# One plain chunk of tokens less, Strassen steps of 1024 tokens, and late weights decoded among the attention heads

## The chip, the core and the metric

The kernel runs on one core of one Trainium2 chip. The metric is the device time of one execution in microseconds (us); lower is better. All arithmetic is in float32, built from pairs of rounded parts as told below.

## What is computed

Causal attention with a decay term for 8 batches of 8 heads, 576 positions and 64 numbers a head, followed by a mixer: one MLP along the positions, one along the channels. Cut to what matters:

```python
scores = q @ k.T / 8 + cum[i] - cum[j]          # cum: running sum of log f; causal
x = (softmax(scores) @ v)                       # 8 batches x 576 tokens x 512 channels
u = x + (relu(x.T @ w_tok1) @ w_tok2).T         # 576 -> 256 -> 576 along the tokens
out = u + relu(u @ w_ch1) @ w_ch2               # 512 -> 1536 -> 512 along the channels
```

There are 8 x 576 = 4608 tokens in the last line. The 1536 hidden channels are 12 tiles of 128.

## The kernel before

**Numbers.** A float32 operand of a matmul is split into a rounded high part and the remainder, the low part (`hi_act`, `lo_dve`, `lo_pool`). A product is then three matmuls: high by high, low by high, high by low. The weights arrive as 64-bit floats; decoding (`decode`, L792) makes float32 of them by one ScalarE operation (L810), a shift (L814) and an OR (L818) on VectorE, and then splits them.

**Heads.** A loop over 64 heads computes scores, softmax and the product with v; after every four heads of a batch `mixer` (L1635) runs the token MLP, and the part of the channel MLP that belongs to the first two hidden tiles (`F1=2`). TensorE, VectorE, ScalarE and GpSimd all work here; GpSimd splits k, q and v and scales the probabilities. The mixed values u and the partial results of the first two hidden tiles go to DRAM (`u_d`, `part_d`).

**Late weights.** The other 10 tiles of w_ch1 and 10 of w_ch2 (`w1r`, `w2r`) don't fit beside the heads' buffers. They are decoded when those buffers are given up (`rest` L867; `gate0`, `gate1`), at the end of the heads.

**Plain chunks.** `CONV=2` chunks of 512 tokens go through these 10 hidden tiles in the ordinary way: `up` (L1238) 12 matmuls of 512 columns for a tile, `down` (L1266) 12 more. Beside them the weights are made ready for the last stage. For each of five pairs of hidden tiles, high and low part of a weight are added again (`prep` L1331, `prep2` L1382), four sums of quarters are formed and split, the sums for w2 are stored in DRAM (`sums_d`), and so are the plain quarters of w2 (`keep` L1373, `quads_d`).

**Strassen steps.** The other 3584 tokens go in four steps of 896 (`big` L1438; `HT=448` is half a step). A step multiplies 2 x 2 blocks with 7 products in place of 8, once up and once down: 7 products x 5 pairs x 6 matmuls each way. The blocks of w1 stay in SBUF; those of w2 are loaded again for every product (`product` L1553), in part into the memory that `w2r` held. The running results R start as the partial results from DRAM plus u (L1472, L1477); for the first step two of their four buffers are those from which the last chunk's output is stored.

**Order.** Nothing is scheduled on the chip: a planner (`Plan`) puts all operations in order ahead of time by priorities (the tables `PR`, by kind of operation, and `prio`), durations and buffers, and each engine works through its own list in order. Operations marked `port=True` on VectorE and all of GpSimd's are planned so that they don't overlap. All DMAs are issued from one queue, SP's, in order.

## Time and profile before

| what | value |
|---|---|
| median of 3 runs | 1040.6 us (1038.58 to 1043.64) |
| the profiled execution, its own time | 1045.64 us |
| its span, first to last instruction | 1043.5 us |
| TensorE busy | 1028.1 us, 99% |
| VectorE busy | 809.2 us, 78% |
| ScalarE busy | 689.8 us, 66% |
| GpSimd busy | 420.2 us, 40% |
| DMA | 192.60 MB, mean 185 GB/s |
| granted TensorE clock, mean | 0.998 of full |

In the profile PE is TensorE's matmuls, PEld its weight loads, DVE is VectorE, ACT is ScalarE, POOL is GpSimd, SP is the queue that issues DMAs. Matmuls overlap, so the distance between the starts of two of them tells their pace, not the duration of one. GpSimd's 420 us all lie in the first 570 us.

### The profile page before, as it was taken

The page shows a single profiled execution, that of the slowest core. Times are in us where ns is not written, and L with a number is a line of the kernel's source. Part 1 is how long each engine was busy: PE and PEld are TensorE (multiplying, and loading weights), DVE is VectorE, ACT ScalarE, POOL GpSimd, SP SyncE. Part 2 cuts the span into 40 slices and gives each one's busy share as a digit, 9 for nine tenths or more (in the row PEclk, how much of TensorE's full clock was granted, in tenths as well). Part 3 has the DMA queues.
Part 4 walks back from the last instruction along what each step waited for, and adds up shares of the span by engine and source line. Part 5 has one row for each costly group of instructions (what it writes and reads, how often), then busy time and mean ns, then how long its engine had stood idle before and what let it go on. Part 6 is the DMA issues. An engine that isn't in the chain of part 4 may idle for free.

```text
span 1043.5 us, 19849 instructions
## 1 busy us (share of the span) xinstructions
PE 1028.1 (99%) x6489; PEld 930.0 (89%) x6489; DVE 809.2 (78%) x1970; ACT 689.8 (66%) x1719; POOL 420.2 (40%) x528
## 2 busy tenths in 40 slices
PE   9999999999999999999999999999999999999998
PEld 7578999999999999999998888879998999999997
DVE  6798888788787868878998895545976886686694
ACT  6888888888888878888996542235454654644652
POOL 6579878778778676977932000000000000000000
PEclk9999999999999999999999999999999999999999
DMA  8765667465564654555657845152582485277054
GB/s 246 246 206 194 217 226 256 162 217 197 189 204 174 219 185 163 196 196 198 225 163 247 267 148 159 47 170 83 167 273 86 135 249 182 81 246 221 18 167 155
DMA packets 101606, 192.60 MB, mean 185 GB/s; under 512 B 14032, under 2 KB 45520, under 8 KB 100480
## 3 DMA queue, kind: packets, MB, share of 16 engines
q1 hardware_dynamic: 101504, 191.34, 55.4%
q8 instruction: 52, 0.85, 0.3%
q14 instruction: 50, 0.41, 0.1%
HBM read 100.16 MB, written 37.49 MB: 132 GB/s over the span
## 4 chain that ended last, share of the span: by engine, by line
PE 87%; DMA 4%; DVE 4%; ACT 2%; issue 1%; SPq 1%; DVEq 0%; ACTq 0%
PE bank L1041 10%; PE bank L985 6%; PE bank L1584 5%; PE bank L1585 5%; PE bank L1586 5%; PE bank L1522 5%; PE bank L1523 5%; PE bank L1524 5%; PE pair L985 3%; PE pair L1123 3%; PE pair L1125 3%; PE pair L1277 2%; PE pair L1279 2%; PE pair L1113 2%; PE pair L1278 2%; DMA dd<-in_w_ch 2%
## 5 line engine op out<-in xcount | busy, mean ns | idle before, releaser
L1027 POOL TENSOR_SCALAR pr<-pr,rec 64x64 f32<-64x64 f32 (+4 forms) x320 | 164.7, 530 | 65.6 <-DVE rec L1020 32.9
L719 ACT ACTIVATE p<-bank 128x384 fp32r<-128x384 f32 (+3 forms) x300 | 130.6, 473 | 20.3 <-PE bank L1041 17.5
L1041 PE MATMUL bank<-ident,pr 128*128 128x128 f32 (+1 forms) x960 | 141.4, 274 | 1.4 <-DVE low L728 0.4
L999 ACT ACTIVATE pr<-bank,nmin 64x64 f32<-64x64 f32 (+3 forms) x256 | 118.2, 468 | 18.4 <-DVE nmin L992 15.7
L1041 PEld LDWEIGHTS bank<-ident,pr 128*128 128x128 f32 (+1 forms) x960 | 106.1, 130 | 19.7 <-issue 2.9
L992 DVE CUSTOM_DVE_ANT_0 bank<-bank,mask 128x320 f32<-128x320 f32 (+3 forms) x256 | 106.8, 433 | 9.3 <-PE bank L985 5.8
L728 DVE TENSOR_TENSOR p<-bank,p 128x384 fp32r<-128x384 f32 (+1 forms) x180 | 105.0, 591 | 10.4 <-ACT p L719 8.7
L985 PE MATMUL bank<-k 128*128 128x320 f32 (+1 forms) x480 | 82.8, 302 | 0.9 <-DVE low L728 0.5
L1584 PE MATMUL bank<-ring,w2r 128*128 128x448 f32 x220 | 80.9, 368 | 2.0 <-DVE h L1539 2.0
L1585 PE MATMUL bank<-ring,w2r 128*128 128x448 f32 x220 | 80.8, 367 | 0.0
L1586 PE MATMUL bank<-ring,w2r 128*128 128x448 f32 x210 | 77.2, 367 | 0.0
L1125 PE MATMUL pair<-p,vv 128*128 128x512 f32 x240 | 76.9, 322 | 0.0
L719 ACT ACTIVATE ring<-xt 128x448 fp32r<-128x448 f32 (+2 forms) x99 | 59.2, 611 | 22.2 <-PE bank L1585 5.2
L911 POOL TENSOR_TENSOR hl<-raw,hl 128x1152 fp32r<-128x1152 f32 x27 | 72.1, 2670 | 1.8
L1123 PE MATMUL pair<-p,vv 128*64 128x512 f32 x240 | 70.4, 334 | 0.0
L728 DVE TENSOR_TENSOR low<-bank,p 64x512 fp32r<-64x512 f32 (+1 forms) x120 | 52.6, 445 | 17.7 <-ACT p L719 15.3
L985 PEld LDWEIGHTS bank<-k 128*128 128x128 f32 (+1 forms) x480 | 62.1, 176 | 4.4 <-ACT pr L999 1.0
L999 ACT ACTIVATE pr<-pair,nmin 128x576 f32<-128x576 f32 x64 | 47.3, 739 | 20.5 <-DVE nmin L992 18.7
L728 DVE TENSOR_TENSOR ring<-xt,ring 128x448 fp32r<-128x448 f32 (+1 forms) x62 | 38.3, 629 | 24.6 <-ACT ring L719 22.9
L992 DVE CUSTOM_DVE_ANT_0 pair<-pair,mask 128x576 f32<-128x576 f32 x64 | 48.9, 764 | 7.0 <-PE pair L985 6.9
L725 POOL TENSOR_TENSOR ring<-xt,ring 128x576 fp32r<-128x576 f32 x32 | 45.8, 1440 | 19.8 <-ACT ring L719 19.4
L722 POOL TENSOR_SCALAR p<-low 64x576 fp32r<-64x576 f32 x60 | 40.4, 673 | 32.2 <-DVE low L728 25.2
(203 smaller groups left out, 3177.9 us busy)
## 6 DMA issues: line engine op xcount, KB each, us to landing
k<-hl SPq DMA_DIRECT2D x180, 288.0 KB
w2r<-sd SPq DMA_DIRECT2D x80, 256.0 KB
raw<-in_qk SPq DMA_DIRECT2D x60, 288.0 KB
w2r<-qd SPq DMA_DIRECT2D x60, 256.0 KB
vr<-in_v SPq DMA_DIRECT2D x32, 320.0 KB
ud<-xt SPq DMA_DIRECT2D x8, 1152.0 KB
pd<-part SPq DMA_DIRECT2D x32, 288.0 KB
dd<-in_w_ch SPq DMA_DIRECT2D x12, 512.0 KB
```

The lines of the kernel that those rows point to most:

```text
L719: nc.scalar.activation(out, in_, func, scale=scale)
L728: nc.vector.tensor_tensor(out, in_, asf(hi), op=ALU.subtract)
L985: nc.tensor.matmul(ps[:m, of : of + w], k[:, 0, i0 : i0 + m], k[:, 1, j0 : j0 + w], start=(x == 0), stop=(fq or x == 1))
L992: nc.vector.tensor_tensor_reduce(x, x, E["mask"][:m, a : a + w], -1.0 / D**0.5, 3e38, op0=ALU.add, op1=ALU.min, accum_out=E["nmin"][sm][:m ...
L999: nc.scalar.activation(at(pr)[:m, poff[t] : poff[t] + w], at(buf)[:m, of : of + w], AF.Exp, bias=E["nmin"][sm][:m, t : t + 1], scale=-1.0, ...
L1027: nc.gpsimd.tensor_scalar(x, x, r, 0.0, op0=ALU.mult, op1=ALU.add)
L1041: nc.tensor.transpose(out, at(pr)[:, poff[i] + start[j] : poff[i] + end[j]], E["ident"])
L1123: nc.tensor.matmul(x[:D], at(vv)[:, v0 + j, :D], at(pb)[:, 1, c0 : c0 + w], start=False, stop=last)
L1125: nc.tensor.matmul(x, at(vv)[:, v0 + j, :], at(pb)[:, 0, c0 : c0 + w], start=False, stop=last)
L1584: nc.tensor.matmul(o_, wh[:, ms], h_, start=first and pr == 0, stop=False, skip_group_check=not first)
L1585: nc.tensor.matmul(o_, wl[:, ms], h_, start=False, stop=False, skip_group_check=not first)
L1586: nc.tensor.matmul(o_, wh[:, ms], l_, start=False, stop=pr == PH - 1, skip_group_check=not first)
```

## The change

It has two parts. `CONV` goes from 2 to 1 and `HT` from 448 to 512: one chunk of 512 tokens is left, and the four steps have 1024 tokens each. And the late weights are decoded among the heads, from the tenth head on, in buffers of the scratch memory `dd`: a pair of w1 tiles is decoded and stored unsplit in DRAM (`g_d`); a pair of w2 tiles is decoded, split and stored (`w2_d`), and its four sums are formed, split and stored at once (`sums_d`). Behind the heads the w1 tiles are loaded and split, the w2 tiles are loaded as they are, and `prep` loads its pairs from `g_d` in place of adding high and low part. `keep` and `quads_d` go; the steps read quarters of w2 out of `w2_d`. The body of `prep2` is otherwise the same. Fewer buffers are left for the steps' split values (16 for 18), and some buffers of the steps lie elsewhere. The tables `PR` have new numbers throughout, and are left out here:

```diff
-HT = 448
-CONV = 2
+HT = 512
+CONV = 1
...
-    def decode(prio, loads, w, hi, lo, tok, late=None):
-        rb, gb = Buf("d_raw"), Buf("d_g")
+    def bits(prio, loads, w, rb, gb, out, wr, dur):
...
-            dma(prio - 1.0, lambda a=(rows, cols, src): ld(*a), nb / len(loads), dur=470 if late else 600, wr=[(rb, i)], bufs=[rb])
+            dma(prio - 1.0, lambda a=(rows, cols, src): ld(*a), nb / len(loads), dur=dur, wr=[(rb, i)], bufs=[rb])
...
+    def prep2(pr, g, prio):
+        e = Buf("pd")
...
+                dma(
+                    prio + 0.6, lambda j=j, z=z, src=src: nc.sync.dma_start(E["sums_d"][pr][:, 2 * j : 2 * j + 2, z, :], src()),
+                    P * C * 4, dur=400, rd=rd, wr=[("st", pr, 2 * j + n, z) for n in (0, 1)], bufs=[g if z else e],
+                )
...
-        def rest(i, which):
+        def rest(pr, w):
             def go(prio):
-                if which == 1:
-                    fs = sl((F1 + i) * P, P)
-                    loads = [(full, sl(c * P, P), w_ch1[sl(c * P, P), fs]) for c in range(NC)]
-                else:
-                    loads = [(full, sl(0, C), w_ch2[sl((F1 + i) * P, P), :])]
-                key = f"w{which}r"
-                decode(
-                    prio, loads, C, lambda: E[key][i][:, 0, :], lambda: E[key][i][:, 1, :], (key, i),
-                    late=f"gate{int(i >= PAIRS0)}",
-                )
+                gb = Buf(f"sg{w}")
+                for j in (0, 1):
+                    i = 2 * pr + j
+                    if w == 1:
+                        fs = sl((F1 + i) * P, P)
+                        loads = [(full, sl(c * P, P), w_ch1[sl(c * P, P), fs]) for c in range(NC)]
+                    else:
+                        loads = [(full, sl(0, C), w_ch2[sl((F1 + i) * P, P), :])]
+                    bits(prio + 1.2 * j, loads, C, Buf("s_raw"), gb, lambda j=j: at(gb)[:, j, :], (gb, j), 470)
+                if w == 1:
+                    dma(prio + 2.4, lambda: nc.sync.dma_start(E["g_d"][pr], asf(at(gb))), P * C * 8, dur=400, rd=[(gb, 0), (gb, 1)], wr=[("g", pr)], bufs=[gb])
+                    return
+                for j in (0, 1):
+                    hb = Buf("sh")
+                    p.op("ACT", d_act(C, False), prio + 2.4, lambda j=j, hb=hb: hi_act(at(hb)[:, 0, :], asf(at(gb)[:, j, :])), rd=[(gb, j)], wr=[(hb, 0)], bufs=[gb, hb])
+                    p.op(
+                        "DVE", d_dve(C), prio + 2.4, lambda j=j, hb=hb: lo_dve(at(hb)[:, 1, :], asf(at(gb)[:, j, :]), at(hb)[:, 0, :]),
+                        rd=[(gb, j), (hb, 0)], wr=[(hb, 1)], bufs=[gb, hb], port=True,
+                    )
+                    dma(prio + 2.4, lambda i=2 * pr + j, hb=hb: nc.sync.dma_start(E["w2_d"][i], asf(at(hb))), P * C * 8, dur=400, rd=[(hb, 0), (hb, 1)], wr=[("w2d", 2 * pr + j)], bufs=[hb])
+                prep2(pr, gb, prio + 3.6)

...
-        third = [rest(i, w) for i in range(F2) for w in (1, 2)]
+        third = [rest(pr, w) for pr in range(F2 // 2) for w in (1, 2)]
...
-        fn(HB + 2 + PRM["DEC3"] * i + (OFF["dec3"] if i < 2 * PAIRS0 else 0.0))
+        fn(10 + 5.2 * i)
+    for i in range(F2):
+        b, gate = Buf("lg"), f"gate{int(i >= PAIRS0)}"
+        pr_ = HB + 2 + 0.5 * i
+        dma(pr_ - 1, lambda b=b, i=i: nc.sync.dma_start(at(b), E["g_d"][i // 2][:, i % 2, :]), P * C * 4, dur=400, rd=[("g", i // 2), ("st", F2 // 2 - 1, 3, 1)], wr=[b], bufs=[b])
+        p.op("ACT", d_act(C, False), pr_, lambda b=b, i=i: hi_act(E["w1r"][i][:, 0, :], at(b)), rd=[b, gate], wr=[(("w1r", i), "h")], bufs=[b])
+        p.op("DVE", d_dve(C), pr_, lambda b=b, i=i: lo_dve(E["w1r"][i][:, 1, :], at(b), E["w1r"][i][:, 0, :]), rd=[b, (("w1r", i), "h")], wr=[(("w1r", i), "l")], bufs=[b], port=True)
+        dma(pr_, lambda i=i: nc.sync.dma_start(asf(E["w2r"][i]), E["w2_d"][i]), P * C * 8, dur=400, rd=[("w2d", i), gate], wr=[(("w2r", i), z) for z in "hl"])
...
-    p.op("POOL", 1, HB + 3, lambda: None, rd=[((f"w{w}r", i), z) for w in (1, 2) for i in range(F2) for z in "hl"], wr=["gated"])
...
-        for j in (0, 1):
-            rd = [((key, i0 + j), z) for z in "hl"] + [("old", key, i0 + j, z) for z in "hl"] + ["gated"]
-            p.op(
-                eng, d(C), prio, lambda j=j: tt(at(g)[:, j, :], asf(E[key][i0 + j][:, 0, :]), asf(E[key][i0 + j][:, 1, :]), ALU.add),
-                rd=rd, wr=[(g, q) for q in QUADS if pos[q][0] == i0 + j], bufs=[g], port=True,
-            )
+        dma(prio - 6, lambda: nc.sync.dma_start(at(g), E["g_d"][pr]), P * C * 8, dur=400, rd=[("g", pr), ("st", F2 // 2 - 1, 3, 1)], wr=[(g, q) for q in QUADS], bufs=[g])
...
-    def keep(pr):
-        for i in (2 * pr, 2 * pr + 1):
-            rd = [(("w2r", i), z) for z in "hl"]
-            for n, hf in ((0, 0),) if i % 2 == 0 else ((1, 0), (2, 1)):
-                dma(
-                    late + PRM["P2"][pr], lambda i=i, n=n, hf=hf: nc.sync.dma_start(E["quads_d"][pr][:, n], asf(E["w2r"][i][:, :, hf * HW : (hf + 1) * HW])),
-                    P * C * 4, dur=650, rd=rd, wr=[("kept", pr, n)],
-                )
...
-        for j in (0, 1):
-            rd = ["gated"] + [(("w2r", i0 + j), z) for z in "hl"]
-            p.op(
-                eng, d(C), prio, lambda j=j: tt(at(g)[:, j, :], asf(E["w2r"][i0 + j][:, 0, :]), asf(E["w2r"][i0 + j][:, 1, :]), ALU.add),
-                rd=rd, wr=[(g, q) for q in QUADS if pos[q][0] == i0 + j] + [("recon", i0 + j)], bufs=[g], port=True,
-            )
...
-    for pr in range(PH):
-        keep(pr)
-    for pr in reversed(range(PH)):
-        prep2(pr, ENG[PRM["E2"][pr]], late + PRM["P2"][pr])
...
-    for nm, a, b, fn in (("gater", 8, 10, lambda: E["swap2"](1)), ("gatew", 0, 8, lambda: None)):
-        p.op("POOL", 1, HB + 3, fn, rd=["gatee", *(("kept", i // 2, n) for i in range(a, b) for n in range(3))], wr=[nm, *((("w2r", i), z) for i in range(a, b) for z in "hl")])
+    for nm, a, b, fn in (("gater", 7, 10, lambda: E["swap2"](1)), ("gatew", 0, 7, lambda: None)):
+        p.op("POOL", 1, HB + 3, fn, rd=["gatee"], wr=[nm, *((("w2r", i), z) for i in range(a, b) for z in "hl")])
...
                 if blk[0] == "A":
-                    tk = [("kept", pr, j)]
+                    i, hf = quad(2, pr, blk[1:])
+                    tk, src = [("w2d", i)], lambda i=i, hf=hf: E["w2_d"][i][:, :, hf * HW : (hf + 1) * HW]
                 else:
-                    tk = [("st", pr, j, z) for z in (0, 1)]
-                d_ = "quads_d" if blk[0] == "A" else "sums_d"
+                    j = dict(S3=0, S1=1, S4=2, S2=3)[blk]
+                    tk, src = [("st", pr, j, z) for z in (0, 1)], lambda j=j, pr=pr: E["sums_d"][pr][:, j]
                 dma(
-                    pp - 16, lambda w=w, d_=d_, pr=pr, j=j: nc.sync.dma_start(asf(at(w)).rearrange("p (z a) -> p z a", z=2), E[d_][pr][:, j]),
+                    pp - 16, lambda w=w, src=src: nc.sync.dma_start(asf(at(w)).rearrange("p (z a) -> p z a", z=2), src()),
                     P * C * 4, dur=650, rd=tk + ["gatew"] * (s == 0), wr=[w], bufs=[w],
...
-    k["tr"] = [(("ring", i),) for i in range(12)] + [(("w2r", i, z),) for i in (5, 6, 7) for z in (0, 1)]
+    k["tr"] = [(("ring", i),) for i in range(12)] + [(("w2r", i, z),) for i in (5, 6) for z in (0, 1)]
     k["tr0"] = k["tr"][:8]
-    k["gw"] = [dd_units(5 * i, 4) for i in (0, 2)]
-    k["pd"] = [tuple(x for i in range(4) for x in dd_units(5 * i + 4, 1))]
+    k["s_raw"] = [dd_units(4 * i, 4) for i in (0, 1)]
+    k["sg1"] = [dd_units(4 * i, 4) for i in (2, 3, 4)]
+    k["sg2"] = [dd_units(8, 4)]
+    k["sh"], k["pd"] = [dd_units(12, 4)], [dd_units(16, 4)]
+    k["lg"] = [dd_units(i, 2) for i in (0, 2, 10, 12)]
...
-    E["quads_d"] = [dram.tile([P, 3, 2, HW], F32, name=f"qd{i}") for i in range((NF - F1) // 2)]
+    E["g_d"] = [dram.tile([P, 2, C], F32, name=f"gd{i}") for i in range((NF - F1) // 2)]
+    E["w2_d"] = [dram.tile([P, 2, C], F32, name=f"wd{i}") for i in range(NF - F1)]
```

## Rows read from the trace of the kernel before

**Rows 1.** The profile's page: span, and busy time of each engine.
```profile
span 1043.5 us, 19849 instructions
PE 1028.1 (99%) x6489; PEld 930.0 (89%) x6489; DVE 809.2 (78%) x1970; ACT 689.8 (66%) x1719; POOL 420.2 (40%) x528
```
**Rows 2.** Busy by stage: stretch, length, busy (instructions), clock, DMA share, GB/s.
```profile
130.00:546.00 416.00, 415.31 (x3200) 393.34 (x3200) 349.09 (x1023) 351.35 (x976) 318.12 (x391) 1.00 0.57 198
546.00:579.30 33.30, 31.20 (x244) 30.02 (x243) 29.78 (x52) 23.13 (x48) 6.11 (x4) 1.00 0.71 236
579.30:690.20 110.90, 110.56 (x487) 90.58 (x487) 74.91 (x156) 35.49 (x79) 0.00 (x0) 1.00 0.44 144
690.20:1038.50 348.30, 345.65 (x1680) 316.10 (x1679) 251.74 (x421) 175.39 (x332) 0.00 (x0) 1.00 0.52 164
```
**Rows 3.** Timeline in a plain chunk: start, duration, instruction; 21 matmuls between.
```profile
654.65 0.39 PE L1257 MATMUL bank<-ring,w1r 128*128 128x512 f32 x1
...
659.64 0.39 PE L1258 MATMUL bank<-ring,w1r 128*128 128x512 f32 x1
```
**Rows 4.** Timeline in a Strassen step; 20 matmuls between.
```profile
895.04 0.36 PE L1524 MATMUL bank<-w2r,w1r 128*128 128x448 f32 x1
...
899.29 0.36 PE L1524 MATMUL bank<-w2r,held 128*128 128x448 f32 x1
```
**Rows 5.** Busy in three stretches of 26 us, the engines as in rows 2.
```profile
416.00:442.00 26.00, 25.88 (x196) 23.28 (x195) 22.96 (x67) 22.54 (x61) 23.67 (x31) 1.00 0.58 198
520.00:546.00 26.00, 26.00 (x202) 24.73 (x201) 24.55 (x64) 24.70 (x62) 11.52 (x19) 1.00 0.52 165
988.00:1014.00 26.00, 26.00 (x129) 24.00 (x128) 25.35 (x47) 13.93 (x27) 0.00 (x0) 1.00 0.41 127
```
**Rows 6.** Instructions grouped by line and shape, VectorE: count, busy us, mean ns.
```profile
L818 DVE SCALAR_TENSOR_TENSOR dd<-dd 128x512 uint32<-128x512 uint32 x22 | 16.0, 737 | 0.3
L814 DVE TENSOR_SCALAR dd<-dd 128x512 uint32<-128x512 uint32 x22 | 11.1, 509 | 3.1 <-ACT dd L810 3.1
L1388 DVE TENSOR_TENSOR dd<-dd 128x256 f32<-128x256 f32 x20 | 8.2, 421 | 0.1
L728 DVE TENSOR_TENSOR dd<-dd 128x256 fp32r<-128x256 f32 x20 | 7.6, 421 | 0.0
L728 DVE TENSOR_TENSOR w2r<-dd,w2r 128x512 fp32r<-128x512 f32 x10 | 6.9, 685 | 0.8 <-ACT w2r L719 0.7
```
**Rows 7.** The same view, ScalarE.
```profile
L810 ACT ACTIVATE dd<-dd 128x512 f32<-128x512 f32 x22 | 14.4, 668 | 4.6 <-DMA dd<-in_w_ch 4.1 <-DVE dd L818 0.4
L719 ACT ACTIVATE dd<-dd 128x256 fp32r<-128x256 f32 x20 | 7.5, 410 | 7.6 <-DVE dd L1388 4.8 <-DVE dd L728 2.6
L719 ACT ACTIVATE w2r<-dd 128x512 fp32r<-128x512 f32 x10 | 6.3, 629 | 3.5 <-DVE dd L818 3.5
```
**Rows 8.** Timeline, GpSimd and VectorE, 557 to 562 us.
```profile
557.60 1.43 POOL L725 TENSOR_TENSOR ring<-xt,ring 128x576 fp32r<-128x576 f32 x1 [11.83 <-ACT ring L719]
559.21 1.42 POOL L725 TENSOR_TENSOR ring<-xt,ring 128x576 fp32r<-128x576 f32 x1 [0.17 <-ACT ring L719]
...
558.33 1.00 DVE L814 TENSOR_SCALAR dd<-dd 128x512 uint32<-128x512 uint32 x1
559.36 1.82 DVE L818 SCALAR_TENSOR_TENSOR dd<-dd 128x512 uint32<-128x512 uint32 x1
```
**Rows 9.** Chain that ended last, end of the heads: start, us, what.
```profile
553.96 3.56 DMA qd<-w2r
...
577.20 5.72 DMA dd<-in_w_ch
```
**Rows 10.** First step: timeline of VectorE and TensorE, and the busy table behind it.
```profile
700.38 1.09 DVE L1477 TENSOR_TENSOR part<-part,xt 128x896 f32<-128x896 f32 x1 [2.18 <-DMA part<-pd]
...
702.11 0.44 PE L1584 MATMUL bank<-ring,w2r 128*128 128x448 f32 x1 [2.01 <-DVE h L1539]
...
703.00:707.00 4.00, 4.00 (x14) 3.55 (x13) 3.16 (x6) 1.56 (x4) 0.00 (x0) 0.60 0.73 238
```

More of the change, by code (lines that the diff above doesn't have):

```diff
@@ L501 @@
     START = dict(PE=3000, DVE=900, ACT=1900, POOL=1810, SP=700)
-    FIFO = ("ring", "xt", "part", "pr", "hl", "k1", "k2", "vv", "raw", "vr", "p34", "p2", "p1", "p0", "low", "hid", "d_raw", "d_g", "tr", "tr0", "gw", "pe", "pd", "wp", "gt12", "gt22", "xu", "qf", "f34", "f2", "f1", "f0")
+    FIFO = ("ring", "xt", "part", "pr", "hl", "k1", "k2", "vv", "raw", "vr", "p34", "p2", "p1", "p0", "low", "hid", "d_raw", "d_g", "tr", "tr0", "s_raw", "sg1", "sg2", "sh", "lg", "pe", "pd", "wp", "gt12", "gt22", "xu", "qf", "f34", "f2", "f1", "f0")
     GROUP = dict(ringx="ring")
@@ L825, in decode @@
-        p.op(
-            "DVE" if late or PRM["ED"] else "POOL", d_dve(w) if late or PRM["ED"] else d_ptt(w), prio, lambda: (lo_dve if late or PRM["ED"] else lo_pool)(lo(), asf(tl()[2]), hi()),
-            rd=[gb, (tok, "h")], wr=[(tok, "l")], bufs=[gb], port=True,
-        )
+        p.op("ACT", d_act(w, False), prio, s1, rd=rd, wr=[wr], bufs=[rb, gb])
+        p.op("DVE", d_dve(w, True), prio, s2, wr=[wr], bufs=[gb], port=True)
+        p.op("DVE", d_dve(w), prio, s3, rd=rd, wr=[wr], bufs=[rb, gb], port=True)
@@ new lines, in decode, with quad @@
+    def decode(prio, loads, w, hi, lo, tok):
+        rb, gb = Buf("d_raw"), Buf("d_g")
+        g = lambda: at(gb)[:, :w]
+        bits(prio, loads, w, rb, gb, g, gb, 600)
+        p.kinds.setdefault("s6", f"k{len(p.kinds)}")
+        p.op("ACT", d_act(w, False), prio, lambda: hi_act(hi(), asf(g())), rd=[gb], wr=[(tok, "h")], bufs=[gb])
+        p.op("POOL", d_ptt(w), prio, lambda: lo_pool(lo(), asf(g()), hi()), rd=[gb, (tok, "h")], wr=[(tok, "l")], bufs=[gb], port=True)
+    def quad(w, pr, q):
+        a, b = int(q[0]) - 1, int(q[1]) - 1
+        return (2 * pr + a, b) if w == 1 else (2 * pr + b, a)
@@ L1987, in swap @@
             for w in (1, 2):
-                pool = tp if w == 2 and i >= 8 else wp
+                pool = tp if w == 2 and i >= 7 else wp
                 E[f"w{w}r"].append(pool.tile([P, 2, C], F32R, name=f"w{w}r{i}"))
         if x == 0:
-            spare = [wp.tile([P, HT], F32, name=f"spare{i}") for i in range(2)]
+            spare = wp.tile([P, HT], F32, name="spare")
             wp.tile([P, 8], F32, name="even1")
@@ L2007, in swap2 @@
             E["H11"] = {tuple(("hid", i) for i in range(PRM["n_hid"])): [tp.tile([P, HT], F32, name=f"h11{i}") for i in range(PH)]}
+            E["H21"][(("hx", 0),)].append(tp.tile([P, HT], F32, name="h212"))
         else:
@@ L2010, in swap2 @@
                 E["R" + q] = {(("w2r", 8 + i),): tp.tile([P, 2 * HT], F32, name=f"r{q}")}
+            E["H21"][(("hx", 0),)].extend(tp.tile([P, HT], F32, name=f"h21{i}") for i in (3, 4))
     top = {}
```

301 lines of the change are left out of this document (145 added, 156 removed).

## The prediction

> **What bounds the kernel now.** I read the busy table first [rows 1]: TensorE is busy 99% of the 1043.5 us span, and no other engine passes 78%. That share is an average and "busy" includes overlapped matmuls, so the next view is the busy table by stage [rows 2]. The reader is to see four stages there. The heads at full pace run from about 130 to 546 us: 3200 matmuls in 416 us, 0.130 us each, TensorE busy 415.3, but VectorE 349.1 (84%), ScalarE 351.4 (84%) and GpSimd 318.1 (76%) beside it. The tail of the heads is 33.3 us. The two plain chunks take 110.9 us, and the four Strassen steps 348.3 us with 1680 matmuls; GpSimd does nothing in both, and VectorE is at 68% and 72%. The granted clock is full in all of them. So TensorE is the bound everywhere, in the heads with little room on the others, after them with much.
>
> Then I read the pace of an undisturbed stream in the timeline. From the 512-column matmul at 654.65 to the one at 659.64 there are 22 steps: 4.99 / 22 = 0.2268 us each [rows 3]. From the 448-column matmul at 895.04 to the one at 899.29 there are 21: 4.25 / 21 = 0.2024 us [rows 4]. 480 x 0.2268 = 108.9 of the 110.9 us of the plain chunks, and 1680 x 0.2024 = 340.0 of the 348.3 us of the steps: both stages are their matmuls, with 2 and 8 us lost.
>
> **The change in matmuls.** A plain chunk is 12 matmuls for the up product and 12 for the down product for each of 10 hidden tiles, 240 of 512 columns. One goes: 240 x 0.2268 = 54.4 us off. A step has 7 products x 5 pairs x 6 matmuls, twice, 420, and four steps 1680, before and after; each grows from 448 to 512 columns: 1680 x (0.2268 - 0.2024) = 41.0 us on. The sum is **-13.4 us**, all on TensorE, which is the path in both stages. It rests on a 512-column matmul in a step running as it does in a chunk: same weight loads, same one bank, so I take it.
>
> [...]
>
> **What the wider step asks of the others.** One column costs VectorE about (685 - 421) / 256 = 1.03 ns [rows 6], so 64 columns add 66 ns to each of the 421 instructions of the steps, some 28 us on 251.7, against 41 on 348.3 for TensorE: its share stays at 72%. Nothing is charged for it. The stretch from 988 to 1014 us had VectorE at 25.35 of 26 us and still passed 129 matmuls [rows 5].
>
> **What moves into the heads.** For each of 20 late weight tiles the three bit operations now run among the heads; so do the split of the 10 w2 tiles, and for five pairs four subtractions and four splits of 256 columns. On VectorE: 20 x 0.737 + 20 x 0.509 (the bits) + 10 x 0.685 (low parts) + 20 x 0.421 + 20 x 0.421 (sums and their low parts) = 14.7 + 10.2 + 6.9 + 8.4 + 8.4 = **48.6 us** in 90 instructions [rows 6]. On ScalarE: 20 x 0.668 + 10 x 0.629 + 20 x 0.410 = 27.9 us [rows 7]. If all of it falls in the 416 us (I subtract nothing for the few decodes that already run at their end), VectorE goes to 397.7 us, 95.6%, and ScalarE to 379.3, 91%. Is that still cover? The nearest row is 520 to 546 us, VectorE 24.55 and ScalarE 24.70 of 26, with 202 matmuls, the mean being 200 [rows 5]: at 94% nothing was lost. Against it speaks 416 to 442, VectorE 22.96 and GpSimd 23.67, with 196: 4 short, about 0.5 us. If all sixteen windows became like that one, 8.3 us would go. Below zero it can't cost, as the change takes no matmul and no evacuation out of the heads. I take the middle, **+4 us**, and keep 0 and 8.3.
>
> All 90 are instructions on SBUF operands, and there is a reason for caution. At 558.33 us a shift took 1.00 us and at 559.36 an OR took 1.82, against means of 0.51 and 0.74; both ended about one ordinary duration after a GpSimd instruction did, the second of these running from 559.21 for 1.42 [rows 8]. So such an instruction can sit out a GpSimd one, and GpSimd is busy 76% of the heads. [...]
>
> **DMA and the SP queue in the heads.** 10.5 MB of raw weights move there, and 13.1 MB of stores are added or moved (5 of 512 KB for the w1 sums' source, 10 of 512 KB for w2, 20 of 256 KB for the sums): 23.6 MB in 416 us, 57 GB/s on 198 and about 0.16 on a DMA share of 0.57. 236 GB/s at 0.71 stands in the next stage [rows 2], so there is room; 85 more issues go through SP, each store waiting there for VectorE with the heads' k and raw loads queued behind it, and TensorE waits for those. The planned order hides it as long as VectorE keeps its place; the cost is zero if so, and part of the second rival if not.
>
> **The end of the heads.** VectorE is busy 29.8 of 33.3 us there, with decoding [rows 2]. That load goes: 244 matmuls at the heads' 0.130 us would take 31.7, so up to 1.6 us could come back. What comes instead is a chain: last store of the sums, load of the decoded w1 tile, its high part, its low part, first matmul. A store took 3.56 us and a load up to 5.72 [rows 9]; with 0.63 and 0.69 for the split that is 10.6 us, and VectorE stands still for what of it isn't covered, with the last head work queued behind. Bounds -1.6 and +5 (half the chain, if TensorE has matmuls in hand for the other half); I take **0**, since the 244 matmuls of the tail mostly belong to heads and mixer and don't wait for late weights.
>
> **One chunk as cover.** A pair of tiles is wanted every 24 x 0.2268 = 5.4 us and brings 0.79 MB, 145 GB/s, under the 236 of the tail. VectorE has, in 54.4 us, some 22 instructions of 0.69, 10 low parts and 40 half-width ones: 15.2 + 6.9 + 16.8 = 38.9 us, 71%. The rebuilding additions and 15 stores vanish; five reloads of 512 KB take their place. I charge nothing. At the first step TensorE waited 2.0 us for a VectorE that waited for the partial sums, and the clock then fell to 0.60 of full for 4 us, 14 matmuls instead of 20, some 1.2 us more [rows 10]. The changed kernel has the same loads behind the same output stores, so this stays: bounds -3.2 and +4, taken **0**. The w2 quarters are read back in two runs instead of one for each row, which no row prices; they are prefetched, so nothing.
>
> **Sum.** -13.4 + 4 + 0 + 0 = -9.4 us. The profiled execution took 1045.6 us, 2.1 of it outside the span, and lies 5.0 over the median of 1040.6, so the difference goes on the median: **1031 us**.
>
> **Rivals.**
> First, *all hidden, and the joints come clean*: heads 0, tail -1.6, the first step's stall gone, -3.2: 1040.6 - 13.4 - 4.8 = 1022. For it: 202 matmuls at 94% VectorE. Against: no stage gets less tight but the tail.
> Second, *VectorE becomes the bound of the heads through the shared port*, the slower case. If each of the 90 waits as the pair did (0.49 and 1.08 over the mean, 0.79) whenever GpSimd is busy, 90 x 0.79 x 0.76 = 54 us. The most VectorE shows anywhere is 25.35 of 26, so 405.6 of 416; it is at 397.7, so it decides from 8 us of added waits, and the gain is gone at 8 + 13.4 - 4, some 17 us of them. At half the bound, 27 us: 27 - 8 = 19 us, plus the 4 already charged: 1040.6 - 13.4 + 23 = 1050. For it: the two long rows, and 90 instructions where that stretch has nearly none now. Against: without the long one the other 21 ORs of this size average (22 x 0.737 - 1.82) / 21 = 0.685 us, the same as a low part; the planned order sets them into GpSimd's gaps.
> Third, *the joints stall*: +5 at the tail and +4 at the first step, 1040, with half the cover in front of the same loads.
> Fourth, *a step's matmul costs by its columns alone*: 0.2024 x 512 / 448 = 0.2313 us, so 1680 x 0.0289 = 48.6 on and a sum of -5.8: 1040.6 - 5.8 + 4 = 1039. Against: a 512-column stream with the same loads runs at 0.2268. [...]
>
> **Chances.** Forecast 0.53 (1027 to 1036), first rival 0.13, second 0.17, third 0.12, fourth 0.05. Range 1021 to 1047: it holds the forecast, the third and fourth, most of the first and the lower edge of the second. 0.5% is 5.2 us, about what a measurement of this kernel can tell from no change. Faster (under 1035.4): 0.13 and most of the forecast, 0.64. Same: the rest of the forecast, the fourth and most of the third, 0.19. Slower: 0.17.
>
> **What would show it.** Right: 240 fewer 512-column matmuls and 1680 at 0.227 us in the steps, steps of some 95 us, one chunk of some 55 us; heads still passing 198 or more matmuls in 26 us with VectorE near 95%. Wrong: fewer than 195 there, long shifts and ORs ending just after a GpSimd instruction (second rival); idle TensorE between the last head and the first chunk matmul, with VectorE waiting for a load (third); a spacing in the steps other than 0.227 (fourth). The prediction falls if the heads end more than 10 us later than before.

## The result, and the profile after

The changed kernel takes **1030.9 us** (median of 4 runs, 1030.01 to 1032.01); the kernel before took 1042.1 (median of 4: the three runs that the forecast started from, and one more of 1044.39). The ratio is 0.9896, with a 95% interval from 0.9863 to 0.9929: faster by about 1%, some 11 us. Forecast were 1031 and a gain of 9.4; against the median of 1040.6 that the forecast started from, the gain is 9.7. In the groups of runs with the experiments the median of the kernel before is 1039.4 to 1040.6. That the time came out nearly to the point is luck, as the stages show.

The page of the changed kernel, to be read against [rows 1]: the span, the busy table, and the shares of the chain that ended last.

```profile
span 1029.7 us, 19321 instructions
PE 1015.0 (99%) x6241; PEld 882.0 (86%) x6241; DVE 804.5 (78%) x1928; ACT 695.8 (68%) x1705; POOL 422.2 (41%) x528
PE 75%; DVE 7%; ACT 6%; DMA 4%; POOL 3%; issue 3%; SPq 2%; ACTq 0%; POOLq 0%; DVEq 0%
```

TensorE is still busy 99%, so the page alone doesn't tell where anything went. The table by stage does. It has the stages of [rows 2]: start, heads at full pace, their tail, the one plain chunk, the four steps (from:to, length, then busy us and instructions of TensorE, weight loads, VectorE, ScalarE, GpSimd, granted clock, DMA share, GB/s).

```profile
0.00:130.00 130.00, 125.28 (x877) 98.86 (x878) 101.86 (x317) 103.43 (x288) 96.40 (x134) 0.99 0.69 225
130.00:558.00 428.00, 423.04 (x3213) 394.06 (x3212) 375.64 (x1101) 363.78 (x1013) 319.68 (x391) 1.00 0.69 240
558.00:586.40 28.40, 27.72 (x218) 26.90 (x217) 19.29 (x38) 17.46 (x35) 6.12 (x4) 1.00 0.77 277
586.40:643.20 56.80, 56.80 (x260) 47.37 (x259) 25.44 (x52) 16.96 (x38) 0.00 (x0) 1.00 0.33 109
643.20:1025.70 382.50, 381.99 (x1682) 314.77 (x1680) 281.62 (x421) 194.22 (x332) 0.00 (x0) 1.00 0.51 158
```

Against [rows 2], profiled execution against profiled execution (spans 1043.5 and 1029.7, 13.9 less before rounding): by the starts of the matmuls, the first of the chunk comes at 586.4 where it came at 579.3, **+7.2**; from it to the first of the steps are 56.9 us where there were 111.0, **-54.1**; from that to the last of the steps 382.1 where there were 348.3, **+33.8**; behind it 0.8 less. The forecast had +4, -54.4 and +41.0. The sum came right through errors of opposite sign: the heads cost more, the steps less. The experiments look for both.

Inside the +7.2 the heads are later still. The last of 768 score matmuls, the fourth of the group in each of these lines, starts at 541.7 instead of 529.1, **12.6 us** late (before, then the changed kernel):

```profile
528.74 0.73 PE L985 MATMUL bank<-k 128*64 128x64 f32 x4
541.36 0.74 PE L1036 MATMUL bank<-k 128*64 128x64 f32 x4
```

Up to there TensorE has passed 3951 matmuls before and 3960 after, and was idle 5.7 and 9.7 us: only 4 of the 12.6 us show as idle time, the rest as matmuls that follow each other more slowly. The spread between profiles matters here: in two more profiles of kernels whose heads are the same (the first experiment and the one on column width) it is 539.4 and 539.1, and the first chunk matmul comes at 583.4 and 583.5: so the last score is 10 to 12.6 us late, the first chunk matmul 4 to 7. From the one to the other before took 50.1 us and the changed kernel 44.7. All this stands against one profile of before, which lies 5 us over its median; if part of that lies in its heads, the differences are larger.

### The profile page after: what moved, and what is told of

Read it like the earlier page. It is cut to its first block, busy times and chain, and to the rows that moved or that the text cites. A ratio compares the mean times of both kernels' runs of the same rounds, so it can differ in the third digit from the quotient of the medians.

```text
span 1029.7 us, 19321 instructions
## 1 busy us (share of the span) xinstructions
PE 1015.0 (99%) x6241; PEld 882.0 (86%) x6241; DVE 804.5 (78%) x1928; ACT 695.8 (68%) x1705; POOL 422.2 (41%) x528
## 4 chain that ended last, share of the span: by engine, by line
PE 75%; DVE 7%; ACT 6%; DMA 4%; POOL 3%; issue 3%; SPq 2%; ACTq 0%; POOLq 0%; DVEq 0%
PE bank L1092 7%; PE bank L1579 6%; PE bank L1580 6%; PE bank L1581 6%; PE bank L1517 6%; PE bank L1518 6%; PE bank L1519 6%; PE bank L1036 4%; ACT pr L1050 2%; PE pair L1036 2%; PE pair L1174 2%; PE pair L1176 2%; PE bank L1758 1%; DMA k<-hl 1%; ACT p L724 1%
## 5 line engine op out<-in xcount | busy, mean ns | idle before, releaser
L1078 POOL TENSOR_SCALAR pr<-pr,rec 128x576 f32<-128x576 f32 (+4 forms) x320 | 166.0, 535 | 61.5 <-DVE rec L1071 39.8
L1050 ACT ACTIVATE pr<-bank,nmin 128x320 f32<-128x320 f32 (+3 forms) x256 | 118.5, 470 | 21.7 <-DVE nmin L1043 20.3
L1092 PEld LDWEIGHTS bank<-ident,pr 128*128 128x128 f32 (+1 forms) x960 | 104.6, 131 | 26.5 <-issue 3.8
L1579 PE MATMUL bank<-ring,w2r 128*128 128x512 f32 x240 | 93.5, 390 | 0.0
L1580 PE MATMUL bank<-ring,w2r 128*128 128x512 f32 x240 | 93.4, 389 | 0.0
L1581 PE MATMUL bank<-ring,w2r 128*128 128x512 f32 x214 | 83.3, 389 | 0.0
L724 ACT ACTIVATE ring<-h 128x512 fp32r<-128x512 f32 x73 | 44.5, 629 | 38.1 <-PE bank L1580 12.7
L724 ACT ACTIVATE ring<-xt 128x512 fp32r<-128x512 f32 (+1 forms) x84 | 53.2, 647 | 23.3 <-DVE xt L1727 7.4
L733 DVE TENSOR_TENSOR low<-bank,p 64x512 fp32r<-64x512 f32 (+1 forms) x120 | 52.2, 441 | 16.2 <-ACT p L724 12.6
L1579 PEld LDWEIGHTS bank<-ring,w2r 128*128 128x128 f32 x240 | 45.0, 188 | 9.7 <-DVE dd L1534 0.3
```

Source lines behind the costliest of these rows:

```text
L724: nc.scalar.activation(out, in_, func, scale=scale)
L733: nc.vector.tensor_tensor(out, in_, asf(hi), op=ALU.subtract)
L1050: nc.scalar.activation(at(pr)[:m, poff[t] : poff[t] + w], at(buf)[:m, of : of + w], AF.Exp, bias=E["nmin"][sm][:m, t : t + 1], scale=-1.0, ...
L1078: nc.gpsimd.tensor_scalar(x, x, r, 0.0, op0=ALU.mult, op1=ALU.add)
L1092: nc.tensor.transpose(out, at(pr)[:, poff[i] + start[j] : poff[i] + end[j]], E["ident"])
L1579: nc.tensor.matmul(o_, wh[:, ms], h_, start=first and pr == 0, stop=False, skip_group_check=not first)
```

## The experiments

The heads are compared below by the start of the last score matmul ("last score") and by number 690 of the 768, in head 57, before the tail begins.

### The old token split, with the late work among the heads

```diff
-HT = 512
-CONV = 1
+HT = 448
+CONV = 2
```

> The changed kernel with the token split of before: halves of 448 columns and two plain chunks, everything else of the change kept, the late weights among the heads too; up to the first chunk's work the order on every engine is that of the changed kernel. Theory, the matmul term of the sum: 240 matmuls of 512 columns come back (+54.4 us) and 1680 lose 64 columns (-41.0), so 13.4 us over the changed kernel, 1030.9 + 13.4 = 1044.3 us, with heads that end as in the changed kernel (last score matmul at 541.7 us) and steps that lose as little as there, 1.3 us over 340. Rival, the losses of before's steps (8.3 us over 340) belong to the 448-column steps or to the two chunks ahead of them: then the stall of 2 us at the first step and the rest come back and it takes 1051. Rival, a step's matmul costs by its columns alone: +5.8, 1036.7 us.

1048.98 us, ratio to before 1.0085 (1.0070 to 1.0101): past the 1044.3 of the theory, and nearer to the 1051 of the first rival. Against the 0.9896 of the changed kernel the new token split is worth 0.0189 x 1040 = 19.7 us, not 13.4. The chunks take 111.3 us there (583.4 to 694.7), as they should, and the steps 348.5, just as in the kernel before. So what was mis-sized lies in the steps: 382.1 - 348.5 = 33.6 us for 64 columns in 1680 matmuls, 0.0200 each. (The other 3 of the 17.4 us between the two profiles are their heads: its first chunk matmul comes at 583.4.) The pace of the 448-column matmuls shows a part of why; the timeline of TensorE in two stretches of this kernel (start, duration, instruction):

```profile
859.70 0.37 PE L1579 MATMUL bank<-ring,w2r 128*128 128x448 f32 x1
859.91 0.37 PE L1580 MATMUL bank<-ring,w2r 128*128 128x448 f32 x1
...
864.66 0.37 PE L1579 MATMUL bank<-w2r,w2r 128*128 128x448 f32 x1
864.87 0.37 PE L1580 MATMUL bank<-w2r,w2r 128*128 128x448 f32 x1
...
1029.62 0.36 PE L1580 MATMUL bank<-ring,w2r 128*128 128x448 f32 x1
1029.82 0.36 PE L1581 MATMUL bank<-ring,w2r 128*128 128x448 f32 x1
...
1034.68 0.36 PE L1581 MATMUL bank<-w2r,w2r 128*128 128x448 f32 x1
1034.89 0.36 PE L1579 MATMUL bank<-ring,w2r 128*128 128x448 f32 x1
```

From 859.70 to 864.87 there are 25 steps, 0.2068 us each; from 1029.62 to 1034.89 there are 26, 0.2027 each. Same shape, same granted clock (1.00 in the stretches from 846 to 872 and from 1014 to 1040 us, with TensorE busy 26.00 of 26 us in both), no wait in either. The stretch of [rows 4] is one of the quick kind. In the steps of the kernel before, 780 of the 1679 spacings lie under 0.2047 us (mean 0.2017), 877 between that and 0.21 (mean 0.2067), and 22 above, which take 9.8 us together. One pace holds over many matmuls, in this run the slower one for some 1000 from 777 to 990 us. In the steps of the changed kernel 1629 of the 1679 spacings of 512-column matmuls lie at 0.226 to 0.228; from 799.91 to 804.67 in the changed kernel there are 21, 0.2267 each:

```profile
799.68 0.39 PE L1581 MATMUL bank<-ring,w2r 128*128 128x512 f32 x1
799.91 0.39 PE L1579 MATMUL bank<-ring,w2r 128*128 128x512 f32 x1
...
804.67 0.39 PE L1579 MATMUL bank<-ring,w2r 128*128 128x512 f32 x1
```

### 64 columns less in the same steps

```diff
-                    q = at(ps)[:, :HT]
+                    q = at(ps)[:, :448]
-                        h_, l_ = at(th[c])[:, :HT], at(tl[c])[:, :HT]
+                        h_, l_ = at(th[c])[:, :448], at(tl[c])[:, :448]
...  (the same for the second product; the first matmul of an accumulation stays at 512)
```

> The changed kernel with the matmuls of the four steps cut from 512 to 448 columns except the first of each accumulation (the last 64 columns of the products get only their first term, the output is another); order, loads, other engines' widths and waits are those of the changed kernel. It prices 64 columns alone. Theory, the pace of the one stretch read before the prediction (0.2024 us): a spacing of 0.2024 in nearly all of the 448-column matmuls, steps of some 344 us where the changed kernel's take 382.3. Rival, a 448-column stream has a second, longer spacing of its own, as the kernel before shows over long stretches (0.2067): part of them at 0.2067, steps of 348 or more, with no stalls to account for it.

1004.43 us, ratio 0.9644 (0.9619 to 0.9669); the steps take 357.5. Of the 1595 spacings of narrowed matmuls 708 lie under 0.2047 (mean 0.2016), 856 between that and 0.21 (mean 0.2065): the second spacing is there in another order, with other loads, so it belongs to the width and not to one order. The rest of the expectation failed: 31 longer spacings take 17.5 us, because VectorE, whose instructions kept 512 columns, now makes TensorE wait (for the additions of line 1534 alone 3.5 us). So this run prices the pace, not the stage. A middle stretch and an undisturbed one:

```profile
736.00:762.00 26.00, 24.71 (x119) 21.89 (x118) 20.50 (x27) 15.49 (x29) 0.00 (x0) 1.00 0.47 148
...
956.00:982.00 26.00, 26.00 (x129) 23.79 (x128) 24.99 (x42) 14.17 (x24) 0.00 (x0) 1.00 0.68 202
```

### The late work's VectorE instructions, cut short

```diff
-            nc.vector.tensor_scalar(g, g, 3, None, op0=ALU.logical_shift_left)
+            nc.vector.tensor_scalar(g[:, :nw], g[:, :nw], 3, None, op0=ALU.logical_shift_left)
...  (nw is 8 for late weights; the same for the OR, the four subtractions and the four low parts)
```

> The changed kernel with 80 of its 90 added VectorE instructions in the heads (20 shifts, 20 ORs, 20 subtractions, 20 low parts of 256 columns) cut to 8 columns, so that these parts of the late weights aren't computed and the output is another; the order on all engines, the transfers and ScalarE's work stay. By their means of 0.41, 0.75, 0.42 and 0.44 us that takes some 40 us off VectorE and leaves about 0.1 us each. Theory A, the heads end 12.6 us later than before because VectorE's added instructions stand in its queue ahead of head work: the last score matmul comes 8 us or more earlier, before 534 us, and the time is 1023 or less. Theory B, the added 23.6 MB and 85 issues of transfers do it: last score within 3 us of 541.7, time 1028 to 1031. Theory C, the new order of the heads' own work does it, whatever the added work costs: the same as B.

1028.05 us, ratio 0.9883 (0.9865 to 0.9901), last score at 540.7. The instructions as they are in the changed kernel, and as they were here, both from the groups of VectorE by line and shape between 130 and 558 us (count, busy us, mean ns, idle before):

```profile
L822 DVE SCALAR_TENSOR_TENSOR dd<-dd 128x512 uint32<-128x512 uint32 x18 | 13.4, 754 | 0.0
L850 DVE TENSOR_TENSOR dd<-dd 128x256 f32<-128x256 f32 x20 | 8.4, 419 | 0.1
L733 DVE TENSOR_TENSOR dd<-dd 128x256 fp32r<-128x256 f32 x20 | 8.2, 437 | 0.0
L818 DVE TENSOR_SCALAR dd<-dd 128x512 uint32<-128x512 uint32 x18 | 7.3, 413 | 0.4 <-ACT dd L814 0.4
```

```profile
L822 DVE SCALAR_TENSOR_TENSOR dd<-dd 128x8 uint32<-128x8 uint32 x18 | 4.0, 231 | 0.0
L850 DVE TENSOR_TENSOR dd<-dd 128x8 f32<-128x8 f32 x20 | 3.2, 160 | 0.1
L733 DVE TENSOR_TENSOR dd<-dd 128x8 fp32r<-128x8 f32 x20 | 3.1, 182 | 0.0
L818 DVE TENSOR_SCALAR dd<-dd 128x8 uint32<-128x8 uint32 x18 | 2.7, 158 | 0.0
```

37.3 us became 13.0: 24 us less, not the 40 of the expectation, since 8 columns still take 0.16 to 0.23 us. (These are sums of durations; the records of neighbouring instructions overlap, and VectorE's busy time between 130 and 542 us fell by 17.7, from 362.6 to 344.9.) But the last score came only 1.0 us forward, less than profiles of the same heads differ (539.1 to 541.7), and theory A, VectorE's added instructions, falls. The first block also answers the fear of long waits for GpSimd: the 18 ORs average 0.754, one of them took 1.88, and the other 17 average (18 x 0.754 - 1.884) / 17 = 0.688, where in the kernel before the ORs without the long one average 0.685; the shifts and subtractions, at 0.413 and 0.419, are no longer than in [rows 6].

### The late work's transfers, cut short

```diff
-            nc.sync.dma_start(o, src...)
+            nc.sync.dma_start(o[few], src...[few])      # 8 of 128 partitions, for four of five pairs
...  (the same for the stores of g_d, w2_d and sums_d)
```

> The changed kernel with the added transfers of four of the five pairs (raw loads of the late weights, stores of decoded, split and summed ones) cut from 128 to 8 partitions, so that four pairs work on the first pair's words and the output is another; all issues, waits and engine work stay where they are, about 18 of 23.6 MB don't move in the heads. Theory A (VectorE): last score matmul within 3 us of 541.7, time 1028 to 1031. Theory B (transfers crowd the heads' own loads): last score before 534 us, time 1023 or less. Theory C (order of the heads' own work): the same as A.

1032.72 us, ratio 0.9930 (0.9915 to 0.9945), last score at 544.2, if anything later (the time is 1.7 past the 1028 to 1031 expected). Between 130 and 542 us the DMA share fell from 0.69 to 0.56 and the rate from 239 to 197 GB/s, about the 0.57 and 198 of before's heads in [rows 2]. Theory B, crowded transfers, falls too. The issues and their waits in SP's queue are still there in this kernel.

### Both cuts, and ScalarE's as well

The first kernel of these joins the edits of the last two; the second adds, for four of five pairs:

```diff
-            nc.scalar.activation(asf(g), asf(high), AF.Prelu, ...)
+            nc.scalar.activation(asf(g[:, :na]), asf(high[:, :na]), AF.Prelu, ...)      # na is 8
...  (the same for the high parts of 512 and of 256 columns)
```

> Both cuts at once in the changed kernel, 80 VectorE instructions to 8 columns and the transfers of four pairs to 8 partitions (most of the late weights' preparation isn't computed, the output is another); order on all engines as in the changed kernel, ScalarE's 28 us stay. Theory A and B: what each alone gives and no more than their sum, last score before 534 us, time 1023 or less. Theory C, the new order of the heads' own work, with ScalarE's part: last score still 538 us or later and the time 1028 or more.

> As the run with both cuts, and ScalarE's added instructions of four of the five pairs (16 of 20 exponent steps, 8 of 10 high parts of 512 and 16 of 20 of 256 columns) and the last low parts of those pairs cut to 8 columns too, so that nearly none of the added work is computed and the output is another; the order on all engines and all issues and waits are those of the changed kernel. By 0.668, 0.629 and 0.410 us that takes some 22 us off ScalarE. Theory C, the new order of the heads' own work costs the 12 us, the added work nothing: last score matmul still 538 us or later, time within 3 us of the run with both cuts (1031). Theory D, it was ScalarE's added work all along: last score before 534 us and the time 1023 or less.

Both cuts: 1031.00 us, ratio 0.9912 (0.9897 to 0.9927), last score at 542.2. With ScalarE's instructions cut too: 1028.06 us, ratio 0.9885 (0.9852 to 0.9917), last score at 538.9. With next to none of the added work done, the heads still end some 10 us later than before. In that last kernel VectorE and ScalarE are busy 343 and 341 of 412 us, no more than the 345 and 348 of before's heads over the same stretch, and TensorE none the less loses its time:

```profile
130.00:542.00 412.00, 406.67 (x3098) 380.31 (x3097) 343.29 (x1071) 341.47 (x987) 313.66 (x383) 1.00 0.57 199
```

That leaves what all these kernels share: the order of the heads' own operations. The change doesn't only insert late work into the queues; its table of priorities is another one throughout, and on each engine about a third of the neighbouring head operations have changed places (on TensorE 334 of 1039 pairs).

### The new order without the work, the old order with and without it

The kernel before, with the heads' operations ranked as in the changed kernel; only the numbers in the table `PR` differ:

```diff
 PR = dict(
-    k24=(...),      # ranks of the heads' operations in the kernel before
+    k24=(...),      # the places in the same queue, filled in the order of the changed kernel
...
```

> The kernel before, with its late weights at the end of the heads as it has them, and the heads' own operations ranked on each engine in the order that they have in the changed kernel. Theory C2: the new order alone costs the heads some 9 us, score matmul number 690 at 486 to 490 us instead of 479.4, last score at 536 to 541 instead of 529.1, time 1046 to 1053. Rival (the order is as good as the other one, and the changed kernel's heads are slow for something else in them): last score within 3 us of 529.1, time within 4 us of before.

1052.9 us, ratio 1.0135 (1.0100 to 1.0170): **the new order alone costs the kernel before 13 to 14 us**. Number 690 comes at 490.1 (expected 486 to 490), the last score at 542.6, 13.5 us later than in the kernel before (expected 536 to 541) and 0.9 later than in the changed kernel, which has the late work on top. Its engines have no more to do than before's (the group of the last score, then the busy table):

```profile
542.21 0.73 PE L985 MATMUL bank<-k 128*64 128x64 f32 x4
...
130.00:542.00 412.00, 406.60 (x3086) 379.29 (x3085) 333.46 (x990) 334.45 (x940) 313.21 (x383) 1.00 0.54 192
```

The other way round, the changed kernel with the old order of the heads and the late work where it was, again by `PR` alone:

```diff
 PR = dict(
-    k24=(...),      # ranks of the heads' operations in the changed kernel
+    k24=(...),      # the heads' places in the same queue, filled in the order of the kernel before
...
```

> The changed kernel with all its work, but the heads' own operations ranked on each engine in the order that they have in the kernel before, the late weights' operations left at the places in the queues that they have in the changed kernel. Theory C (the order of the heads' own work costs the 12 us): last score matmul between 529 and 534 us, where before has 529.1, and a time of 1019 to 1024, below both kernels. Rival (the heads can't take the late work without some 10 us, in whatever order): last score at 538 us or later, time 1028 or more.

1035.93 us, ratio 0.9949 (0.9931 to 0.9968): slower than the changed kernel, with number 690 at 494.8 and the last score at 545.0. My theory in its first form, that the old order would have taken the late work for nothing, falls. Two kernels with the late work held back until head 56 complete the four cases:

```diff
+    p.writer["late"] = [next(o for o in p.ops if o.grp == ("k24", 56))]
     for i, fn in enumerate(third):
         fn(10 + 5.2 * i)
...
-            dma(prio - 1.0, ..., dur=dur, wr=[(rb, i)], bufs=[rb])
+            dma(prio - 1.0, ..., dur=dur, rd=["late"] if dur == 470 else [], wr=[(rb, i)], bufs=[rb])
```

> The changed kernel with the raw loads of the late weights held back until head 56 of 64 has its sums, so that decoding, summing, splitting and the stores run at the end of the heads and behind them, with everything else of the change kept. It prices the move into the heads by undoing it. Theory C in the form that the late work costs the heads little by itself: last score matmul within 3 us of 541.7 since the heads' own work keeps its ranks, and then a wait of TensorE for the late weights: 10.5 MB of raw loads and 13 MB of stores at the 236 GB/s of before's tail are some 100 us from about 485 us on, and a load and split of 6.4 us behind them, so a first chunk matmul at 590 to 640 us where the changed kernel has 586.4, and 1035 to 1085 us. Rival, room made for the late work costs the heads 12 us: last score at 533 us or earlier.

> As the run that held the late weights back until head 56, with the heads' own operations ranked in the order of the kernel before instead of the changed kernel's: the missing one of four cases (two orders, late work in the heads or out of them). By the score matmul number 690 of 768, of head 57, the other three stand 9.8 us (changed order, late work in), 8.7 (changed order, out) and 15.4 (order of before, in) behind the kernel before. Theory C2, the order costs the time, the one made round the late work as well as the one into which it is put afterwards, and nothing in the buffers or addresses of the changed kernel does: number 690 within 2 us of before (477 to 481 us). Rival (something else in the changed kernel's heads slows them, whatever the order): 6 us or more behind. The end of the heads and the time are again those of late weights that come too late, above 1080 us.

They take 1107.3 us (ratio 1.063, 1.0592 to 1.0667) and 1106.6 (1.0648, 1.0601 to 1.0694), since the first chunk matmul waits for the weights until 661.2 and 660.3, well beyond the 590 to 640 expected: undone, the move into the heads costs some 75 us with one chunk. What they were made for is number 690, in us behind the kernel before:

| order of the heads' own operations | late work out of the heads | late work in the heads |
|---|---|---|
| as before | +2.9 | +15.4 |
| as changed | +8.7 | +9.8 |

Each cell is one profile, and profiles of the same heads differ by up to 2.6 us there (489.2 in the changed kernel, 486.9 with the old token split, 486.6 in the run on column width). The +2.9 is 0.9 over the 2 us that I had allowed, and below the 6 of the rival: buffers and addresses of the changed kernel can make up a part of its delay at most. In the new order the late work costs 9.8 - 8.7 = 1.1 us, less than profiles differ; in the old one it costs 15.4 - 2.9 = 12.5. So the late work is nearly free in an order that leaves room for it, and it is that order which costs the heads most of the 10 us: 8.7 - 2.9 = 5.8 us between the two kernels with late work out of the heads, and 490.1 - 479.4 = 10.7 in the kernel before. The planner doesn't keep to the ranks quite: in these kernels the heads' operations stand on average up to 0.5 of a place from the order that was asked for, where the two orders are 1.6 to 2.0 places apart. The last scores, 546.3 and 537.4, can't be read like that, as the decoding begins ahead of them; the first is 4.5 behind the changed kernel's where 3 were allowed.

### Three times the OR

```diff
-            nc.vector.scalar_tensor_tensor(g, low, 29, g, ...)
+            for _ in range(3 if dur == 470 else 1): nc.vector.scalar_tensor_tensor(g, low, 29, g, ...)
```

> The changed kernel with each of the 20 late ORs issued three times in a row (the same result each time), order otherwise unchanged: 40 instructions of 0.754 us, 30 us more on VectorE, which goes from 362.6 to some 390 of 412 us between 130 and 542, 95%, the share that the prediction reckoned with. Theory A' (the prediction's bounds, 0 to 8.3 us for a VectorE at 95%): last score matmul 0 to 8 us after 541.7, time 1028 to 1037 on a chip where before takes 1040. Rival, at 95% each added instruction delays the head work behind it: 15 us or more, last score after 555, time above 1043.

1071.44 us, ratio 1.0306 (1.0268 to 1.0345), last score at 581.7: **40.0 us later, for 29.7 us more of VectorE** (54 ORs, 43.1 us, where 18 took 13.4). The share of 95% never came: VectorE is busy 396.8 of 452 us, 88%, between 130 and 582, TensorE 423.6. From the start to the last score, over the same 3960 matmuls, TensorE is idle 38.6 us instead of 9.7, so 29 of the 40 us are idle time; the other 11 are slower matmuls, as the granted clock is 0.98 there on the mean instead of 1.00. One place in the timeline shows how it goes (the brackets: idle before, and what ended it):

```profile
337.46 2.12 DVE L822 SCALAR_TENSOR_TENSOR dd<-dd 128x512 uint32<-128x512 uint32 x3
339.51 0.81 DVE L733 TENSOR_TENSOR low<-bank,p 64x512 fp32r<-64x512 f32 x2
340.24 0.66 PE L1092 MATMUL bank<-ident,pr 128*128 128x128 f32 x4 [1.90 <-DVE low L733]
```

The three ORs hold VectorE's queue for 2.12 us; the low part of the next probabilities stands behind them, and TensorE stands 1.90 us for that. Each engine works through its list, so here a delay is passed on to the engine that is next in the plan, though VectorE is at 88%. The list itself was planned for single ORs.

## Why the prediction was right, and where it was not

**Plain chunk.** 240 matmuls at 0.2268 were 54.4 us; the chunk stages differ by 54.1. Right.

**Wider steps: the mis-sized term.** 1680 x 0.0244 = 41.0 became 33.8. What failed is the price of the old width, the 0.2024 of [rows 4]: a true stretch, but one of two kinds, and without the waits. The prediction had the better number on its table, 348.3 us for 1680 matmuls, 0.2073 each [rows 2], and split it into 340.0 of pace and 8.3 "lost". Against a uniform 0.2024 x 1679 = 339.8, the normal spacings of before hold 3.2 us more and the 22 long ones 5.3 more; the changed kernel loses 1.3 against 0.2268 x 1680. So 7 of the 8.3 us went away with the 448 columns: about 3 by the pace, the rest by waits. Of the 5.3 us in long spacings 3.8 are the first step's stall and the low clock behind it (0.60 over 4 us in [rows 10]), which the forecast kept and the first rival took off at 3.2. In the run with the old split the same sum came back in other parts: 4.5 us by the slower pace, which held for 1155 spacings there, and 4.1 in 12 long ones, none of them a stall of 2 us. That the two kernels have the same 348.3 and 348.5 is in part chance. In the changed kernel the step's stall is indeed gone: VectorE still waits for the partial results, as in [rows 10], but the first matmul of line 1579 follows without a wait (TensorE's one wait in that step, 0.5 us, comes at 655.7):

```profile
652.62 1.23 DVE L1472 TENSOR_TENSOR part<-part,xt 128x1024 f32<-128x1024 f32 x1 [1.63 <-DMA r<-pd]
652.85 0.39 PE L1579 MATMUL bank<-ring,w2r 128*128 128x512 f32 x1
```

The runs price 64 columns at 226.7 - 202.7 = 24.0 ns from the quick spacing and at 226.7 - 206.8 = 19.9 from the slow one.

**Heads.** +4 was taken, between 0 and 8.3, for VectorE at 95%. Both halves of that step failed. VectorE is at 375.6 of 428 us, 88%: its busy time rose by 26.5 us and not by 48.6, as some 44 us of the added instructions lie in that stretch, some 8 of late decoding were in it before, and overlapping records count once. The heads end 10 to 12.6 us later by the last score, at or past the bound of 10 that the prediction set itself; 24 mixer matmuls that now run ahead of it (below) make that 7 to 9.4. In 4 of the 16 stretches of 26 us from 130 us on TensorE passes fewer than 195 matmuls (190 to 194 in them, the lowest here), the mark for the second rival, but without that rival's cause: no queue of long shifts, one OR of 18 that took long, 1.88 us at 337.8 us.

```profile
338.00:364.00 26.00, 24.87 (x190) 23.40 (x190) 23.20 (x64) 19.89 (x57) 16.07 (x19) 1.00 0.82 277
```

The reasoning from a share of busy time to a cost was the error. Cutting 24 us from VectorE left the heads' end where it was, within the spread of profiles, and adding 30 put it 40 back, so neither slope can be read from "94% and nothing lost" in [rows 5]. What the term left out is the new order of the heads' own work, which alone costs 6 to 11 us by score 690. That waits for GpSimd and the transfers cost nothing to speak of was right, by the cut kernels.

**Second rival.** It didn't happen, but its price was too low: it decided "from 8 us of added waits", where in this order 30 us of added VectorE time cost 40, so that little or none of it is free. The 8 came from 25.35 of 26 us as the most that VectorE shows anywhere; the kernel before has 25.82, with 128 matmuls, from 746 to 772 us. Such waits are in the traces, and the "port" of the rival's name stands for no more than these: in the changed kernel the OR of 1.88 us began at 337.83, a GpSimd instruction ran from 338.03 for 1.15, and the OR ended 0.53 us after that one; in the kernel before, the OR of [rows 8] ended 0.55 us after its GpSimd instruction. What in the chip makes them wait no run shows.

**End of the heads.** Taken 0, between -1.6 and +5. Of the 5.5 us that the stretch from the last score to the first chunk matmul is shorter, 24 mixer matmuls of some 0.133 us that the new order does earlier are 3.2, and these belong to the heads' account; some 2.3 are a gain, a little past the lower bound. The chain that was feared is there and covered. ScalarE waits for the first decoded tile until 558.4, one load takes 8.09 us, more than the 5.72 reckoned with, and the first chunk matmul follows the mixer's last at 586.43:

```profile
558.42 1.32 ACT L724 ACTIVATE w1r<-dd 128x512 fp32r<-128x512 f32 x2 [0.86 <-DMA dd<-gd]
...
565.68 8.09 DMA dd<-gd
...
586.29 0.30 PE L1788 MATMUL bank<-ring,held 128*128 128x288 f32 x1
586.43 0.39 PE L1314 MATMUL bank<-ring,w1r 128*128 128x512 f32 x1
```

**One chunk as cover.** Right: TensorE is busy all of the 56.8 us, at a DMA rate of 109 GB/s, with VectorE busy for 25.4 of them where 38.9 were reckoned.

**The sum.** Heads and tail +7.2 for +4 (4 to 7 over three profiles), steps +33.8 for +41.0, chunk -54.1 for -54.4, the end -0.8: -13.9 in the profiles and 10 to 11 us off in the medians, for -9.4. The profile of before lies 5 us over its median, and which stage has them isn't known. What stays open is why the new order is slower, operation by operation; the runs show that it is the order, and that the old one is no better with the late work in it. An order as quick as before's that also has room for the late work would be worth an estimated 7 to 9 us more (10 to 12.6 less the 3.2 of the mixer matmuls), and wasn't found here.

## What to carry to other kernels

Price a stage by its whole length over its matmuls before you price it by a clean stretch, and look at a second and third stretch: a shape can have two paces, as 448 columns had here (0.2027 and 0.2068 us), and "losses" may be the slower one. Where every engine works through a list fixed ahead, as here, the share of busy time priced neither work put in nor work taken out; the price of moving work under other work was here that of the new order, and it was measured by running the new order without the work. When a forecast meets the time, check its terms against the stages all the same: here errors of 3 and 7 us partly hid each other.

## What the runs showed of the hardware

Matmuls of 448 columns, each with a new weight load of 128 x 128 (1679 loads for 1680 matmuls in [rows 2]), ran at two spacings at a granted clock of 1.00, 0.2027 and 0.2068 us in the two stretches of the run with the old split, while 512 columns ran at 0.2267 in the changed kernel. What picks one or the other is not settled: a pace held for hundreds of matmuls, 1027 at the longest, and of six changes in the kernel before and in the run with the old split four came behind a late matmul, but two, at 993 and at 990 us, did not.

VectorE instructions of 8 columns took 0.16 (shift, subtraction), 0.18 (low part) and 0.23 us (OR) where 256 or 512 columns took 0.41 to 0.75: 31 to 42% of the time is left when nearly all columns are gone.

In the run with three ORs TensorE was busy for 0.44 of the 4 us from 124 to 128; the granted clock was 1.00 in the first two of these, 0.67 in the last two and 0.50 in the two behind them, by the table of stretches of 2 us:

```profile
122.00:124.00 2.00, 1.82 (x13) 1.34 (x11) 1.97 (x4) 1.52 (x4) 1.92 (x2) 1.00 0.02 5
124.00:126.00 2.00, 0.00 (x0) 0.00 (x0) 1.97 (x2) 0.00 (x0) 1.32 (x1) 1.00 0.00 0
126.00:128.00 2.00, 0.44 (x3) 0.37 (x4) 2.00 (x9) 0.87 (x4) 0.00 (x0) 0.67 0.14 47
128.00:130.00 2.00, 2.00 (x10) 1.87 (x9) 1.00 (x4) 1.74 (x7) 0.00 (x0) 0.50 0.89 274
```
